# An attention and two-feed-forward kernel on one core: k and q of the first 512 tokens loaded four tokens to a packet, w_out scaled by row, partition maxima turned on DVE

## The chip, the cores and the metric

The kernel runs on 1 core of one Trainium2 chip. The metric is the device time of one execution in microseconds, the median of several runs. TensorE is called PE in the profile (its weight loads PEld), VectorE DVE, ScalarE ACT, GpSimd POOL, SyncE SP.

## What is computed

Four batches of 768 tokens, 8 heads of 64, go through a local attention with 8 memory rows a head, then a gated layer, then a layer with softmax gating and a normalisation. FP32 in and out; the weights come as FP64.

```python
for c in range(nc):                       # chunks of 32 tokens
    k_ctx = k[:, :, c*32-16 : c*32+32+8]  # cut at both ends of the sequence
    k_full = concatenate([mem_k, k_ctx]); v_full = concatenate([mem_v, v_ctx])
    a = softmax(q_c @ k_full.T / 8)
    out[:, :, c*32 : c*32+32] = a @ v_full
x = out as (3072, 512)
y = (sigmoid(x @ w_gate) * (x @ w_val)) @ w_out        # 512 -> 1536 -> 512
h = y @ w_in                                           # 512 -> 1024
solu = h * softmax(h)
out = layernorm(solu) * g_ln @ w2_out                  # 1024 -> 512
```

## The kernel before, in words

The 3072 tokens are 24 tiles of 128 tokens, and 6 blocks of 4 tiles (`j`). There are three stages. In the first, attention makes x of the tiles, and the products with w_gate and w_val run per block over 12 pieces `m` of 128 columns (`up`, line 625: two groups of 12 matmuls with 512 columns, each FP32 product being three with parts `h` and `l`); g = sigmoid times val goes out to DRAM (`gd`). In the second, g comes back and is multiplied with w_out (`down`, line 717). In the third come h (`prod`, line 770, seven products of a two-by-two scheme), the gating and normalisation, and the last product (`out_mm`, line 860).

Attention of a tile `t`: k and q come token by partition (`d_load`, line 472: a descriptor for each token and head, 64 FP32), TensorE turns them four times each with `ident` (`d_turn`, line 456), ACT evicts k into windows of a chunk's 56 tokens plus 8 memory columns (`d_kev`, line 484: three copies) and q (`d_qev`, line 504). POOL copies what neighbours share (`d_halo`) and the memory columns (`d_kmem`). `two_banks` (line 515) makes 32 small matmuls for the scores; DVE takes maximum and difference (`a_max`, lines 530 and 531), ACT the exponential, DVE the sum and its reciprocal (`a_sum`, lines 538 to 540), TensorE turns the result (`d_p`), ACT evicts it (line 547), `two_banks` multiplies with v, DVE divides (`d_norm`, line 593), TensorE turns it (`d_x`), and ACT and DVE split it into `xh` and `xl` (lines 606, 610). v comes as overlapping windows of two tiles (`d_v`, lines 563 to 570), and their tails, the memory rows of v, from a DRAM copy that repeats them eight times (`d_vexp`, `d_vm`, line 582). mem_k is loaded and turned once for each of the four batches (`d_mload`, `d_mem`).

A weight piece is a DMA of 512 KB in 1 KB packets (`w_load`, line 418), an ACT pass for the exponent (`w_exp`, line 214), three DVE operations for the bits (`f32_bits`, lines 219 to 223), an ACT copy for the high part (line 279) and a POOL subtraction for the low one (line 230). w_out also gets a scale: `wo_max` on DVE, `wo_spread` (line 434, an all-reduce over partitions on POOL), `wo_set`. `gm_spread`, `p_spread` and `w2i_spread` are all-reduces too.

The order is not written by hand: `Plan` holds a task for each step with engine, duration, buffers and due times, and lists them all. `SHIFTS` names seeds that move due times at random. Each engine and each DMA queue then runs its list in order.

## Time and profile before

| | us |
|---|---|
| median of 3 runs | 946.63 (945.9 to 946.66) |
| span of the profiled execution, first to last instruction | 944.6 |
| its own time beside the span | not printed; median less span is 2.0 |
| PE busy | 915.7 (97%) |
| DVE busy | 609.3 (65%) |
| ACT busy | 426.6 (45%) |
| POOL busy | 89.2 (9%) |

The profile has the busy time of each engine, the span in slices with the granted clock and the DMA share, the chain of waits that ended last, and groups of instructions by line with what ended the idle time ahead of them. "issue" as releaser means that the profile shows nothing that was waited for. Below, rows of these views are shown word for word.

### The profile page before, as it was taken

Reading aid. Unit: us, or ns where it says so; the run is one execution under the profiler, and the core shown is the slowest. Engines: PE = TensorE matmul, PEld = TensorE weight load, DVE = VectorE, ACT = ScalarE, POOL = GpSimd, SP = SyncE. Lnnn points to the kernel's source line nnn. Section 1 sums busy time; section 2 is a strip of 40 time slices with the busy share of each in tenths; the row PEclk is TensorE's granted clock in tenths of the full one; section 3 lists DMA queues with packets and bytes.
Section 4 is the critical chain, followed back from the end, with each engine's and each line's share of the span. In section 5 each row is a group of like instructions: output and inputs, shape, how many; then the busy total and the mean of one; then the engine's idle time right before and its main releaser. Section 6 shows DMA issues by size and latency. Waiting matters only on the chain.

```text
span 944.6 us, 17813 instructions
## 1 busy us (share of the span) xinstructions
PE 915.7 (97%) x7144; PEld 593.3 (63%) x7144; DVE 609.3 (65%) x1097; ACT 426.6 (45%) x690; POOL 89.2 (9%) x154
## 2 busy tenths in 40 slices
PE   5599999999999999999999999999999999999998
PEld 4487778888888878888787444444444444444443
DVE  3599856656666676677647357783783773777581
ACT  4367632622742462264244245553552633554452
POOL 1143320000100000000006100000000000000000
PEclk9799999999999999999999999999999999999999
DMA  9999997794485557343772532344244144232323
GB/s 175 273 182 219 210 229 243 161 195 152 130 196 172 158 124 199 114 128 122 243 277 85 172 90 78 79 112 101 59 110 101 56 121 94 70 96 45 78 67 101
DMA packets 201746, 132.64 MB, mean 140 GB/s; under 512 B 152768, under 2 KB 167104, under 8 KB 201664
## 3 DMA queue, kind: packets, MB, share of 16 engines
q1 hardware_dynamic: 191424, 105.29, 45.1%
q10 hardware_dynamic: 10240, 26.22, 8.9%
q8 instruction: 56, 0.92, 0.4%
q14 instruction: 26, 0.21, 0.1%
HBM read 86.38 MB, written 33.03 MB: 126 GB/s over the span
## 4 chain that ended last, share of the span: by engine, by line
PE 86%; DVE 5%; DMA 5%; issue 1%; ACT 1%; SPq 1%; POOL 0%; ACTq 0%; DVEq 0%
PE u L625 35%; PE y L717 20%; PE ps L860 13%; PE Q L770 5%; PE tr L456 4%; PE R L770 3%; PE P L770 3%; PE ps L515 3%; DMA r<-in_moe_w_val_dram 2%; DVE w L220 1%; DVE w L223 1%; DVE w L219 1%; DVE pl L401 1%; DMA rk<-in_k_dram 1%; DMA vw<-mv 1%
## 5 line engine op out<-in xcount | busy, mean ns | idle before, releaser
L625 PE MATMUL u<-xh,wa 128*128 128x512 f32 x1152 | 371.1, 396 | 5.1 <-ACT wa L279 1.8
L625 PEld LDWEIGHTS u<-xh,wa 128*128 128x128 f32 x1152 | 216.9, 188 | 53.0 <-ACT sg L631 2.3
L625 PE MATMUL u<-xl,wa 128*128 128x512 f32 x576 | 225.1, 391 | 0.0
L717 PE MATMUL y<-gh,pl 128*128 128x512 f16 x576 | 177.4, 379 | 0.0
L717 PEld LDWEIGHTS <-pl 128*128 128x128 f16 x864 | 84.4, 98 | 102.0 <-issue 0.3
L860 PE MATMUL ps<-wo,nt 128*128 128x512 f16 x576 | 127.6, 379 | 0.8 <-ACT o L867 0.8
L625 PEld LDWEIGHTS u<-xl,wa 128*128 128x128 f32 x576 | 108.7, 189 | 21.4 <-DVE xl L610 0.2
L442 ACT ACTIVATE gh<-gi,gm 128x512 f16<-128x512 f32 x72 | 51.7, 720 | 131.3 <-PE y L717 124.0
L717 PE MATMUL y<-gl,pl 128*128 128x512 f16 x288 | 109.2, 379 | 0.0
L232 DVE SCALAR_TENSOR_TENSOR gl<-gi,gm,gh 128x512 f16<-128x512 f32 x72 | 53.6, 750 | 82.1 <-ACT gh L442 81.9
L860 PEld LDWEIGHTS <-nt 128*128 128x128 f16 x576 | 56.4, 98 | 68.9 <-issue 1.1
L631 ACT ACTIVATE sg<-u 128x512 f32<-128x512 f32 x72 | 42.9, 595 | 123.0 <-PE u L625 108.2
L636 DVE TENSOR_TENSOR g<-sg,u 128x512 f32<-128x512 f32 x72 | 49.3, 685 | 72.9 <-PE u L625 49.4
L770 PEld LDWEIGHTS <-yh 128*128 128x128 f16 x336 | 32.9, 98 | 39.6
L829 POOL TENSOR_TENSOR ls<-ls,mhalf 128x1 f32<-128x1 f32 x24 | 15.4, 645 | 355.4 <-DVE ls L825 355.4
L214 ACT ACTIVATE w<-r 128x512 f32<-128x512 f32 x46 | 30.4, 666 | 36.3 <-DMA r<-in_moe_w_gate_dram 9.5
L770 PE MATMUL Q<-pl,yh 128*128 128x512 f16 x144 | 42.8, 379 | 0.0
L291 DVE TENSOR_REDUCE gm<-g 128x1 f32<-128x512 f32 x60 | 40.9, 681 | 1.7
L219 DVE TENSOR_SCALAR w<-w 128x512 int32<-128x512 int32 x52 | 27.4, 527 | 22.3 <-ACT w L214 22.1
L791 DVE TENSOR_TENSOR pl<-Q,pl 128x512 f32<-128x512 f32 x36 | 24.7, 687 | 23.7 <-PE Q L770 23.6
L230 POOL TENSOR_TENSOR wa<-w,wa 128x512 fp32r<-128x512 f32 x24 | 31.9, 1331 | 76.7 <-ACT wa L279 76.7
L803 ACT ACTIVATE e<-pl,ls,few 128x1024 f32<-128x1024 f32 x24 | 29.7, 1239 | 19.1 <-DVE ls L797 11.8
(122 smaller groups left out, 1112.1 us busy)
## 6 DMA issues: line engine op xcount, KB each, us to landing
gd<-g SPq DMA_DIRECT2D x72, 256.0 KB
gi<-gd SPq DMA_DIRECT2D x72, 256.0 KB
r<-in_moe_w_out_dram ACTq DMA_DIRECT2D x28, 512.0 KB
vw<-in_v_dram SPq DMA_DIRECT2D x64, 98.0 KB
rk<-in_k_dram SPq DMA_DIRECT2D x24, 256.0 KB
...
```

Of the source, the lines that this page charges most:

```text
L219: nc.vector.tensor_single_scalar(out=d, in_=d, scalar=3, op=ALU.logical_shift_left)
L230: nc.gpsimd.tensor_tensor(out=dst, in0=x, in1=hi, op=ALU.subtract)
L232: nc.vector.scalar_tensor_tensor(out=dst, in0=x, scalar=s, in1=hi, op0=ALU.mult, op1=ALU.subtract)
L291: nc.vector.tensor_reduce(out=dst, in_=a, axis=AX.X, op=ALU.max, apply_absolute_value=True)
L442: nc.scalar.activation(out=dst, in_=x, func=AF.Copy, scale=s)
L456: nc.tensor.transpose(pv[:, kk, :], src[:, 2 * kk:2 * kk + 2, :], ident[0:rows, 0:rows])
L625: nc.tensor.matmul(u, lhsT=a, rhs=c[:, kk, w[0]:w[1]], start=(n == 0), stop=(n == 3 * KM - 1))
L631: nc.scalar.activation(out=sg, in_=U.pop((j, m, 0, w)), func=AF.Sigmoid)
L636: nc.vector.tensor_tensor(out=g, in0=U.pop((j, m, "s", w)), in1=U.pop((j, m, 1, w)), op=ALU.mult)
L717: nc.tensor.matmul(y, lhsT=a, rhs=c, start=(f == 0 and n == 0), stop=(f == MF - 1 and n == 2))
L770: nc.tensor.matmul(ps, lhsT=yc[a][:, c, kk, u * 128:(u + 1) * 128], rhs=t[:, hl, kk, :], start=(first and n == 0), stop=(n == 5), skip_gro ...
L860: nc.tensor.matmul(ps, lhsT=nt[:, a, kk, :], rhs=C["wo2"][:, c, kk, :], start=(n == 0), stop=(n == 3 * K2 - 1))
```

## The change

- k and q of tiles 0 to 3 (batch 0, 512 tokens) come in two DMAs each, with four tokens of a head side by side in a partition (1 KB). TensorE turns each head and each of the four tokens with a plain matmul against `ident` (64 columns of weights), not a transpose; the eviction, half on ACT and half on DVE, puts the tokens in order by its read pattern. `kT` windows of these tiles are then full, and `d_halo` has nothing to do for them.
- The first weight pieces stand ahead of v. mem_k of all batches is loaded at once, from ACT's queue, and turned once. The tails of v are made by way of SBUF.
- v gets a 65th column of ones, so the product gives the row sum; `a_sum` is gone, `d_norm` makes the reciprocal.
- w_out's scale is its maximum by row, without the spread; the maxima over all partitions that are left (8) are made by `across` on DVE in 13 small instructions.
- The three DVE steps of a weight piece are tasks of their own; pieces 0 to 19 use four buffers in a place that a later weight takes. `SHIFTS` and due times differ, and `START` sets the first order.

```diff
-    SHIFTS = [(4001, 2), (4002, 0.5), (4006, 0.5), (4010, 2), (4039, 2), (4069, 2), (4114, 1)]
+    SHIFTS = [(2754, 1), (8610, 0.5), (5405, 2), (8526, 0.3), (363, 0.5), (4604, 0.5)]
...
+        for x, n in enumerate(first):
+            T[n]["due"] = x - 100.0
...
-    def wo_spread(f):
-        spread(PF[:, f:f + 1], PF[:, f:f + 1])
-
...
-    def spread(a, dst):
-        nc.gpsimd.partition_all_reduce(dst, a, 128, ReduceOp.max)
+    def across(a):
+
+        nc.vector.tensor_copy(turn[:, 0, 0:1], a)
+        nc.vector.transpose(turn[:, 1], turn[:, 0])
+        nc.vector.tensor_reduce(out=turn[:, 0, 1:2], in_=turn[:, 1], axis=AX.X, op=ALU.max)
+        for x in range(1, 4):
+            nc.vector.tensor_copy(turn[0:1, 0, 1 + x:2 + x], turn[32 * x:32 * x + 1, 0, 1:2])
+        nc.vector.tensor_reduce(out=turn[0:1, 0, 5:6], in_=turn[0:1, 0, 1:5], axis=AX.X, op=ALU.max)
+        for x in range(4):
+            nc.vector.tensor_copy(turn[32 * x:32 * x + 1, 1], turn[0:1, 0, 5:6].to_broadcast([1, 32]))
+        nc.vector.transpose(turn[:, 0], turn[:, 1])
+        nc.vector.tensor_copy(a, turn[:, 0, 0:1])
...
     def d_mload(b):
-        nc.sync.dma_start(out=mm[0:NM], in_=mem_k[b].rearrange("h p d -> p h d"))
+        nc.scalar.dma_start(out=mm[b * NM:(b + 1) * NM], in_=mem_k[b].rearrange("h p d -> p h d"))
...
+    def f_load(nm):
+        R[nm] = xp.tile([128, H, 4, D], F32, tag=dict(rk="xh", rq="xl")[nm], name=nm)
+        src = dict(rk=k, rq=q)[nm][0, :, 0:512, :].rearrange("h (g e) d -> g h (e d)", e=4)
+        for x in range(2):
+            hh = slice(4 * x, 4 * x + 4)
+            nc.sync.dma_start(out=R[nm][:, hh].rearrange("p h e d -> p h (e d)"), in_=src[:, hh])
+
+
+    def f_turn(ps, nm, kk):
+        for e in range(4):
+            for x in range(2):
+                out_ = ps[D * x:D * x + D, e * 128:(e + 1) * 128]
+                nc.tensor.matmul(out_, lhsT=R[nm][:, 2 * kk + x, e, :], rhs=ident, start=True, stop=True)
...
+    def f_kev(t, x):
+        copy = nc.vector.tensor_copy if x else nc.scalar.copy
+        for kk in (2 * x, 2 * x + 1):
+            ps = PS["fk", kk]
+            base = 32 * t - LC // 4
+            for c, n, z in ((0, 1, 10), (1, 3, 14)) if t == 0 else ((0, 3, 14), (3, 1, 12)) if t == 3 else ((0, 4, 14),):
...
+                copy(out_, src)
...
-    def a_sum(t):
-        rs = RS[t] = sm.tile([128, H], F32, tag="rs", name="rs", bufs=4)
-        nc.vector.tensor_reduce(out=rs, in_=SS[t], axis=AX.X, op=ALU.add)
-        nc.vector.tensor_single_scalar(out=rs, in_=rs, scalar=1e-9, op=ALU.add)
-        nc.vector.reciprocal(out=rs, in_=rs)
...
-            w = VW[n] = tp.tile([128, KM, 8, D], F32, tag="vw", name="vw")
+            w = VW[n] = tp.tile([128, KM, 8, D + 1], F32, tag="vw", name="vw")
+            nc.gpsimd.memset(w[..., D:D + 1], 1.0)
...
     def d_norm(t):
...
-        nc.vector.tensor_tensor(out=out_, in0=PS.pop((t, 2)), in1=rs, op=ALU.mult)
+        rs = rs.unsqueeze(3).to_broadcast([128, 2, KM, D])
+        nc.vector.tensor_tensor(out=out_, in0=ps[..., 0:D], in1=rs, op=ALU.mult)
...
+    def gm_top(j):
+        nc.vector.tensor_tensor(out=GM[:, j], in0=GM[:, j], in1=PF, op=ALU.mult)
+        nc.vector.tensor_reduce(out=FH[j], in_=GM[:, j], axis=AX.X, op=ALU.max)
...
+    START = ["vfill", "rk4", "vone"] + [("mload", b) for b in range(B)] + [
+        "rq4", ("dvexp", 0), ("wld", 0), ("wld", 1), ("dv", 0, 0), ("dv", 0, 1), ("dvm", 0), ("rk", 4),
+        ("dv", 1, 0), ("dv", 1, 1), ("dvm", 1), ("wld", 2), "vtwo", ("dvexp", 1)]
```

TensorE's order before, from the start of the program (`rk` and `rq` are k and q by token, `tr` the turned result, `mm` mem_k, `ps` scores or the product with v, `s` the softmax; a count is that of the program, where a plain FP32 matmul stands once):

```order
L456 MATMUL tr<-ident,rk 128x128 x8
L456 MATMUL tr<-ident,mm 128x32 x4
L456 MATMUL tr<-ident,rq 128x128 x8
L515 MATMUL ps<-kT,qT 32x64 x32
L456 MATMUL tr<-ident,rk 128x128 x8
L456 MATMUL tr<-ident,s 128x128 x4
L456 MATMUL tr<-ident,rq 128x128 x4
L515 MATMUL ps<-kT,qT 32x64 x64
L456 MATMUL tr<-ident,rk 128x128 x4
L456 MATMUL tr<-ident,s 128x128 x4
L456 MATMUL tr<-ident,rq 128x128 x4
L515 MATMUL ps<-kT,qT 32x64 x32
```

The same now, twelve rows; eight transposes more and the weight products follow (`fq` is q of the four tiles, in order):

```order
L491 MATMUL tr<-ident,rk 64x128 x32
L491 MATMUL tr<-ident,rq 64x128 x32
L460 MATMUL tr<-ident,mm 128x32 x4
L574 MATMUL ps<-kT,fq 32x64 x96
L460 MATMUL tr<-ident,rk 128x128 x4
L460 MATMUL tr<-ident,s 128x128 x8
L574 MATMUL ps<-kT,fq 32x64 x32
L574 MATMUL ps<-vw,pT 32x65 x32
L460 MATMUL tr<-ident,s 128x128 x4
L574 MATMUL ps<-vw,pT 32x65 x64
L460 MATMUL tr<-ident,s 128x128 x12
L574 MATMUL ps<-vw,pT 32x65 x32
```

The first sixteen transposes of k and q become 64 plain matmuls in one run ahead of everything, and the scores of three tiles follow in one run.

SP's queue before, from the start (`vw` v's windows, `mv` the repeated memory rows of v, `r` a weight piece):

```order
L472 DMA rk<-in_k_dram 128x8x64 x2
L472 DMA rq<-in_q_dram 128x8x64
L460 DMA mm<-in_mem_k_dram 8x8x64
L472 DMA rq<-in_q_dram 128x8x64
L563 DMA vw<-in_v_dram 40x4x64
L570 DMA vw<-in_v_dram 56x7x64 x4
L472 DMA rk<-in_k_dram 128x8x64 x2
L472 DMA rq<-in_q_dram 128x8x64
L577 DMA mv_189<-in_mem_v_dram 512x1x64
L563 DMA vw<-in_v_dram 40x4x64
L570 DMA vw<-in_v_dram 56x7x64 x4
L472 DMA rk<-in_k_dram 128x8x64
```

And now:

```order
L484 DMA rk<-in_k_dram 128x4x256 x2
L484 DMA rq<-in_q_dram 128x4x256 x2
L410 DMA r<-in_moe_w_gate_dram 128x4x256
L410 DMA r<-in_moe_w_val_dram 128x4x256
L617 DMA vw<-in_v_dram 40x4x64
L624 DMA vw<-in_v_dram 56x7x64 x4
L617 DMA vw<-in_v_dram 40x4x64
L624 DMA vw<-in_v_dram 56x7x64 x4
L648 DMA vw<-mv_175 8x4x520 x2
L476 DMA rk<-in_k_dram 128x8x64
L624 DMA vw<-in_v_dram 56x8x64 x8
L648 DMA vw<-mv_175 8x4x520 x2
```

k and q are four issues where they were eight; the first two weight pieces stand ahead of v where they stood behind most of it.

DVE's order now, from its eviction of tiles 1 and 2 on (`wf` a weight piece, `mk` mem_k, `gm` here the maxima of the scores; L527 is the eviction of k, L510 that of q):

```order
L527 COPY kT<-tr 128x4x56 x4
L220 TENSOR_SCALAR wf<-wf 128x512
L223 SCALAR_TENSOR_TENSOR wf<-r,wf 128x512 x2
L510 COPY fq<-tr 128x1024
L470 COPY mk<-tr 128x128
L220 TENSOR_SCALAR wf<-wf 128x512
L223 SCALAR_TENSOR_TENSOR wf<-r,wf 128x512 x2
L586 MEMSET ps 32x2x4x16
L589 TENSOR_REDUCE gm<-ps 128x2x4
L590 TENSOR_TENSOR s<-ps,gm 128x2x4x64
```

Before, DVE began with two memsets, mem_k's copy and the first tile's maximum; two weight pieces and half the evictions now stand ahead of that.

## Rows read from the trace of the kernel before

**Rows 1.** Windows: engines' busy us (instructions), granted clock, DMA share, GB/s, by stage

```profile
0.00:44.40 44.40, 24.61 (x585) 18.50 (x585) 18.54 (x38) 18.32 (x42) 5.24 (x23) 0.88 1.11 222
44.40:130.00 85.60, 82.84 (x875) 67.25 (x876) 74.14 (x114) 54.58 (x101) 33.46 (x40) 0.98 0.95 207
130.00:510.00 380.00, 379.12 (x3705) 309.27 (x3704) 248.15 (x468) 153.12 (x255) 25.19 (x62) 1.00 0.60 171
```

**Rows 2.** Timeline of PE, 4 to 45 us: start, duration, line, count, idle before, releaser

```profile
4.20 2.23 PE L456 MATMUL tr<-ident,rk 128*128 128x128 f32 x8 [4.20 <-DMA rk<-in_k_dram]
...
14.71 1.06 PE L456 MATMUL tr<-ident,s 128*128 128x128 f32 x4
...
18.99 0.32 PE L515 MATMUL ps<-kT,qT 64*32 64x64 f32 x8 [0.77 <-issue]
...
20.37 0.60 PE L456 MATMUL tr<-ident,s 128*128 128x128 f32 x4
...
22.87 0.85 PE L515 MATMUL ps<-kT,qT 64*32 64x64 f32 x64 [0.82 <-ACT qT L504]
...
25.93 0.64 PE L515 MATMUL ps<-vw,pT 64*32 64x64 f32 x39 [0.23 <-DMA vw<-mv]
29.13 0.65 PE L515 MATMUL ps<-vw,pT 64*32 64x64 f32 x23 [2.56 <-issue]
...
36.83 0.48 PE L515 MATMUL ps<-vw,pT 64*32 64x64 f32 x33 [3.03 <-issue]
...
39.40 1.11 PE L456 MATMUL tr<-ident,s 128*128 128x128 f32 x4
...
44.39 0.77 PE L625 MATMUL u<-xh,wa 128*128 128x512 f32 x1 [1.82 <-ACT wa L279]
```

**Rows 3.** Waits of PE, whole run: total us, times, longest

```profile
PE ps L515 <- issue: 6.4, 3, 3.0
```

**Rows 4.** Page, parts 1 and 3: TensorE's instructions, and the queue of instruction packets

```profile
PE 915.7 (97%) x7144; PEld 593.3 (63%) x7144; DVE 609.3 (65%) x1097; ACT 426.6 (45%) x690; POOL 89.2 (9%) x154
...
q8 instruction: 56, 0.92, 0.4%
```

**Rows 5.** DMA queues in one-us stretches from 15.5, 25.5, 33.5, 40.5 us: packets, MB, share

```profile
q8 instruction: 1, 0.02, 9.3%
q8 instruction: 1, 0.02, 8.0%
q8 instruction: 1, 0.02, 7.2%
q8 instruction: 1, 0.02, 7.1%
```

**Rows 6.** Windows of 2 us, columns as in rows 1

```profile
16.00:18.00 2.00, 2.00 (x122) 1.59 (x122) 0.47 (x1) 1.12 (x3) 0.00 (x1) 1.00 1.33 167
38.00:40.00 2.00, 2.00 (x69) 1.55 (x68) 0.60 (x2) 0.58 (x1) 0.00 (x0) 0.50 1.09 348
```

**Rows 7.** Timeline of SP's queue and ACT, 20 to 28 us

```profile
20.12 0.71 SPq L582 DMA_DIRECT2D vw<-mv  x2
20.88 0.39 SPq L418 DMA_DIRECT2D r<-in_moe_w_gate_dram  x1
...
27.44 0.66 ACT L214 ACTIVATE w<-r 128x512 f32<-128x512 f32 x1 [4.19 <-DMA r<-in_moe_w_gate_dram]
```

**Rows 8.** Groups of DVE by form: busy us, mean ns of one, idle before

```profile
L220 DVE SCALAR_TENSOR_TENSOR w<-r,w 128x512 int32<-128x512 int32 x46 | 33.7, 733 | 1.6
...
L531 DVE TENSOR_TENSOR s<-ps,smx 128x512 f32<-128x512 f32 x24 | 16.6, 692 | 0.8
...
L538 DVE TENSOR_REDUCE rs<-s 128x8 f32<-128x512 f32 x24 | 16.1, 671 | 3.2 <-ACT s L534 3.2
...
L438 DVE TENSOR_SCALAR pf<-pf 128x1 f32<-128x1 f32 x12 | 1.8, 151 | 3.8 <-POOL pf L434 3.8
```

**Rows 9.** Timeline of PE at the second batch's mem_k

```profile
77.03 0.43 PE L456 MATMUL tr<-ident,mm 32*128 32x32 f32 x4
```

More of the change, by code (lines that the diff above doesn't have):

```diff
@@ L7 @@
 from concourse._compat import with_exitstack
-from concourse.bass_isa import ReduceOp
 from concourse.masks import make_identity
@@ L44, in add, with order @@
         )
-    def order(self):
+    def order(self, first):
         T = self.tasks
@@ L170, in encoder_kernel, with column @@
     const = ctx.enter_context(tc.tile_pool(name="const", bufs=1))
+    turn = const.tile([128, 2, 32], F32, name="turn")
+    tiny = const.tile([128, 2 * MF + 4 * K2 + 18], F32, name="tiny")
+    ends = [0]
+    def column(n):
+        ends.append(ends[-1] + n)
+        return tiny[:, ends[-2]:ends[-1]]
+    gcol, PM, PW, GS = (column(K2) for x in range(4))
+    PF, SF = column(MF), column(MF)
+    fo, mhalf, few = column(1), column(1), column(16)
     wpool = ctx.enter_context(tc.tile_pool(name="wpool", bufs=1))
@@ L179, in encoder_kernel @@
     dr = ctx.enter_context(tc.tile_pool(name="dr", bufs=1, space=DRAM))
-    gcol = const.tile([128, K2], F32, name="gcol")
-    fo = const.tile([128, 1], F32, name="fo")
-    mk = [const.tile([128, KM, NM], F32, name=f"mk{b}") for b in range(B)]
     FIRST_IN = {6: ("w", 0), 8: ("w", 1), 10: ("w", 2)}
@@ L189, in encoder_kernel @@
     FIRST_TAGS = {f"wa{m}" for m in FIRST_IN}
-    wa = [None if m in FIRST_IN else wpool.tile([128, 2, 2, 512], F32R, name=f"wa{m}") for m in range(MF)]
+    WF = 20
+    FIRST_TAGS |= {f"wa{MF - 1}", f"wa{MF - 3}"}
+    wa = [None if f"wa{m}" in FIRST_TAGS else wpool.tile([128, 2, 2, 512], F32R, name=f"wa{m}") for m in range(MF)]
     def slot(x, shape, dt=F32):
@@ L888, in one @@
             prev=(nm, t - 1), **kw)
-    add("zero", POOL, 0.5, d_zero)
     add("ident", POOL, 0.7, d_ident)
     for b in range(B):
-        one("mload", b, SP, 0.1, d_mload, [("dmem", b - 1) if b else "zero"], dma=[0.09])
-        one("dmem", b, PE, 0.3, d_mem, ["ident", "mload"], acq=[("u0", ("dm", b))])
-        one("dmev", b, DVE, 0.3, d_mev, ["dmem"], rel=[("u0", ("dm", b))])
+        one("mload", b, ACT, 0.1, d_mload, dma=[0.09], acq=[] if b else [("g", "mm")])
+    add("dmem", PE, 0.3, d_mem, deps=["ident"] + [("mload", b) for b in range(B)], acq=[("a", "dm")], rel=[("g", "mm")])
+    add("dmev", DVE, 0.2, d_mev, deps=["dmem"], rel=[("a", "dm")])
     for n in range(NTILE // 2):
@@ new lines, in encoder_kernel @@
+        one("dhalo", t, POOL, 0.6, d_halo, after + ([("dhalo", t - 1)] if i else []) + ([("dkev2", 3)] if t == 4 else []))
+        one("dkmem", t, POOL, 0.45, d_kmem, after + ["dmev"])
+        one("sw", t, PE, 0.85 if early else 0.75, d_scores,
+            (["fqev0", "fqev1", "dkev", "dkev2"] if early else ["dqev"]) + ["dkmem", ("dhalo", t if i == TB - 1 or t < 3 else t + 1)],
+            acq=[("a", t), ("s", t)], rel=[("kT", t)] + ([("qT", t)] if t > 3 else [(f"wa{MF - 3}", "early")] if t == 3 else []), slack=0 if t < 6 else SLACK)
@@ L963, in encoder_kernel @@
             continue
-        one("wexp", n, ACT, 0.68, w_exp, ["wld"], acq=[("w", n)])
-        one("wbits", n, DVE, 2.2, w_bits, ["wexp"], rel=rel)
-        one("whi", n, ACT, 0.62, w_hi, ["wbits"], acq=[(f"wa{m}", m)] if m in FIRST_IN and n % 2 == 0 else [])
-        one("wlo", n, POOL, 1.4, w_lo, ["whi"], rel=[("w", n)])
+        buf = [("wf" if n < WF else "w", n)]
+        one("wexp", n, ACT, 0.68, w_exp, ["wld"], acq=buf + ([(f"wa{MF - 1}", "wf")] if n == 0 else []))
+        for x, y in enumerate(("wsh", "wlow", "wbits")):
+            one(y, n, DVE, (0.46, 0.74, 0.74)[x], lambda n, x=x: w_bits(n, x), [("wexp", "wsh", "wlow")[x]], rel=rel if x == 2 else [])
+        one("whi", n, ACT, 0.62, w_hi, ["wbits"], acq=[(f"wa{m}", m)] if f"wa{m}" in FIRST_TAGS and n % 2 == 0 else [])
+        one("wlo", n, POOL, 1.4, w_lo, ["whi"], rel=buf + ([(f"wa{MF - 1}", "wf")] if n == WF - 1 else []))
     for f in range(MF):
@@ L1033, in encoder_kernel @@
     add("gcol", SP, 0.1, lambda: nc.sync.dma_start(out=gcol, in_=g_ln.rearrange("(k p) -> p k", p=128)), dma=[0.1])
-    add("mhalf", DVE, 0.07, lambda: nc.vector.memset(mhalf, -0.5))
+    add("turn", DVE, 0.07, lambda: nc.vector.memset(turn, 0.0), due=0.1)
+    add("mhalf", DVE, 0.07, lambda: nc.vector.memset(mhalf, -0.5), due=0.1)
+    add("warm", ACT, 0.2, warm, deps=["mhalf"], table="exp", due=1.0)
     add("w2done", "mark", 0, lambda: None, deps=[("tlo", c) for c in range(7)])
@@ L1127, in encoder_kernel @@
         plan.tasks[n]["due"] = clock
+    line = [n for n in START if plan.tasks[n]["eng"] == SP]
+    for a, b in zip(line, line[1:]):
+        plan.tasks[b]["prev"] = a
+    plan.tasks["rq4"]["prev"] = ("mload", B - 1)
     ctx.enter_context(tc.manual_schedule())
-    for part in plan.order():
+    for part in plan.order(START):
         part["fn"]()
```

207 lines of the change are left out of this document (125 added, 82 removed).

## The prediction

> **What bounds the kernel now.** I read the stages first, then TensorE's own order, then what ended its idle time. By stages [rows 1], TensorE is busy 82.8 of the 85.6 us from 44.4 to 130 and 379.1 of the 380 up to 510; the weight products fill it from 44.4 us on. In the first 44.4 us it works 24.6, though the DMA engines are full (a share of 1.11). So the place where the change can pay is the road to the first weight product, which starts at 44.39 [rows 2]. I call that moment T0. What shortens it comes off the end one for one, since after it nothing but TensorE's own work sets the end; what the change saves on DVE, ACT or POOL later is cover.
>
> What holds T0? Three lines of TensorE end idle time put down to "issue", in which nothing the profile follows is waited for: 0.77 us before 18.99, 2.56 before 29.13, 3.03 before 36.83 [rows 2]. They cut a run of equal matmuls in the middle, and TensorE's list of waits has no others of the kind in the whole run [rows 3]. Counted over all lines of that stretch, 220 pairs of weight load and matmul stand before the first stop, 125 more before the second, 126 more before the third. The page gives 7144 pairs and, on the queue named "instruction", 56 packets of 0.92 MB, 16.4 KB each [rows 4]: 7144 / 56 = 127.6 pairs to a packet. So TensorE's program comes in pieces of some 126 pairs, and these are the stops where the next piece was not there. Such packets are seen in the one-us stretches that begin at 15.5, 25.5, 33.5 and 40.5 [rows 5]: each of the first three ends some 2.5 to 3 us before the matmul that waited. From the start of one piece to the start of the next, a piece took 18.99 to 29.13 = 10.1 us and 29.13 to 36.83 = 7.7; the one before took 4.3 (its predecessor began, by the count, near the line at 14.71). I call this a refill.
>
> The rest of the time before T0 is data. Packets of 256 B, of which k, q and v come (64 FP32 of a head and token), move 167 GB/s, the 1 KB packets of the weights 348 [rows 6]. The small tail of v issued at 20.12 lets the first product with v begin at 25.93, and the first weight piece, issued at 20.88, is used at 27.44 [rows 2, 7].
>
> **The change, part by part.** Load: k and q of tiles 0 to 3 are 2.1 MB; at 167 GB/s that is 12.6 us of the engines, at 348 6.0, so 6.6 us less in front of v and the weights. Laid end to end in SP's new order, with 2 us to the first bytes: k and q 6.0, weights 0 and 1 3.0, the small loads 1, v of the first pair with its tail 1.0 MB 6.0, a k tile 1.6, v of the second pair 1.0 MB 6.2; v of tiles 2 and 3 is in near 26. I allow 1 us to land: 27. It serves the third product, the old counterpart of which went on at 36.83.
>
> Turning: 32 transposes of 128 columns go, 64 plain matmuls with 64 columns of weights come. Plain FP32 matmuls stand twice in the trace (64 pairs of them for a tile, 32 in the program), so 128 pairs replace 32. No row shows one. A transpose takes 0.60 / 4 = 0.15 us at full clock, 1.11 / 4 = 0.28 at 39.40, where the granted clock is 0.50, the 1.2 GHz of the two levels [rows 2, 6]. Below, they cost what the 32 did, 4.8 us; above, each pair costs a whole transpose, 19.2. I take half of the latter, 9.6, because each fills half the columns: from 4.2 (where the first turn starts now [rows 2]) to about 14. The evictions of k and q, now ACT's, become halves on ACT and DVE; six halves at 0.69 [rows 8], 4 us, come to DVE before T0, where it is busy 18.5 of 44.4 [rows 1].
>
> Scores, maximum and exponential of four tiles: DVE needs two operations of 0.69 a tile plus two weight pieces of three operations near 0.73 [rows 8], which the new order puts ahead of the first maximum. Laid in a row, scores of tile 1 run near 16.5 and those of tile 3 near 22.5, the last product with v near 28, and then its division (0.69 and two small ones), a transpose of 0.6 and the copy that feeds the weight product, with DVE's other work between: T0 near 33 by the engines alone; by the data, 27 and the 7.56 from 36.83 to 44.39, it is 34 to 35. I take 34 for both.
>
> The refills come in again there. By the count, 584 pairs lie before T0 now and 680 then (96 more). The pieces' ends at 220, 345, 471 and 596 pairs fall in tile 1's scores (16.5), early in tile 3's scores, at the start of the second product with v, and right behind the third. **Three refills thus stand between 16.5 and the last stretch, where now two do.** What one takes in the new traffic isn't shown; its ends are 4.3 and 10.1. I take 6.0: nearer the low end, since from 26 us on only 1 KB packets are queued, and under those the packet at 40.5 to 41.5 [rows 5] starts at most 4.7 us after 36.83. Three give 16.5 + 18.0 = 34.5; the last stretch (two transposes, a product of 0.85 or more [rows 2], a division, a transpose, a copy) 5.0: **T0 = 39.5**, 4.9 us earlier.
>
> The rule that speaks here is in the Trainium skill, DMA: Bandwidth & Descriptors, section Queues, rings and completion order: each DMA engine takes the queues that have work in turn, packet by packet. By that a refill would wait for a packet or so and never for the backlog, and T0 would be 34; the rows with 7 us between 18.99 and the packet's stretch from 25.5 do not look like it. This is the first rival.
>
> After T0: three turns of mem_k go (once for all batches), 0.43 each, a little of it under what follows: 1.1 off [rows 9]. The ones column makes 65 columns of 64 in the products of 20 later tiles; between nothing and 1/64 of 0.85 each, I take 20 x 0.013 = 0.3 on. The row sums leave DVE, 24 x 0.67 = 16 us; 20 all-reduces leave POOL, and 8 turns come to DVE, 13 small instructions each. At 0.15, a small one of the present [rows 8], that is 16 us; its ends are nothing and, at 0.69, 72. All under TensorE: from 130 to 510 us DVE is idle 132 of 380 [rows 1], so the upper end is covered too unless it sits in one place. Six DMAs go to ACT's queue ahead of its first copy; that copy can't come before the first turns end, past 5 us, so nothing. SP's tail of v now waits for mem_v to go to SBUF and out to DRAM, and a k tile and the second v stand behind it; some 8 us for two trips against a turn at 12 or later: nothing.
>
> Sum on the profiled execution: 944.6 - 4.9 - 1.1 + 0.3 = 938.9. Its span is 944.6, the median of the runs 946.63, so 2.0 lie around it: **940.9**. What a measurement of this kernel can tell from no change is 0.2%, 1.9 us.
>
> **The rivals.** *Refills never late.* They wait for a packet, not a queue; then T0 = 34 and 944.6 - 10.4 - 0.8 + 2.0 = 935.4. For: behind 36.83 no stop follows [rows 3], though TensorE goes on through its pieces. Against: three in the first 37 us. If the 2.8 us that TensorE idles from 44.4 to 130 shrink too, 932.6; this is the low end, with 1.6 for a quicker turning. 0.25.
>
> *Weights late.* T0 moves, but from 44.4 to 130 DVE works 74.1 of 85.6 [rows 1] at weight pieces and four tiles, so the block ends no sooner than DVE lets it: four row sums, 2.7, and the 0.8: 943.1. Against: TensorE is the fuller of the two. 0.07.
>
> *Refills as now.* The mean of the three is 7.4; four of them from the turning's first piece end (9.8) and the last stretch give 9.8 + 29.6 + 5.0 = 44.4: T0 stays, and 945.8. 0.18.
>
> *Slower: refills as the longest.* The 96 added pairs put one more refill in the road. At 10.1 each, T0 = 9.8 + 40.4 + 5.0 = 55.2, and 956.6. It decides from 8.2 us a refill on, where T0 is 47.6 and the time 949. For it: the longest is the one in a queue of v's 256 B packets, and v is what is queued when the third is due. Against: two of three were shorter, and weights fill the queue by then. 0.14, most of it just past the point.
>
> **How the numbers follow.** The forecast case has 0.36, and with it the others give faster 0.36 + 0.25 + 0.07 = 0.68, same 0.18, slower 0.14. The range takes in the first rival with its low end and reaches up to the point where the last begins to decide, 931 to 949; about 0.15 is outside. The faster cases alone span 931 to 944.
>
> **What would show it.** Right: T0 at 38 to 41; SP's k and q by 9 us at some 340 GB/s; stops put down to "issue" 125 pairs apart, four of them, before T0; refill packets that precede them by 3 us; TensorE full from T0 on with its busy time within 1 us of now after it. Wrong: no such stops before T0 (first rival), T0 at 44 or later with stops of 4 us and more (the last two), or idle TensorE between T0 and T0 + 70 put down to ACT or POOL at the weights (the second). A turning of over 15 us would break the step on its price, TensorE waiting for v near 30 us that on the load. A stop in the later blocks at the small DVE turns would break the cover.

## The result, and the profile after

The changed kernel takes **960.33 us** (median of 4 runs, 956.95 to 965.35); the kernel before, beside it on the same chip, 946.64 (945.90 to 947.54). The ratio is 1.0143, interval 1.011 to 1.0176: 1.4% slower, where 940.9 was forecast. The profiled execution took 956.95 with a span of 954.7, so 2.3 us lie around it; it is the fastest of the four. Two executions below, one of the changed kernel in another order (1060.41 us) and one of the kernel before (1055.23), ran at a granted clock of 0.84 and are left out of the ratios.

The stages, with the columns of [rows 1]:

```profile
0.00:44.40 44.40, 25.24 (x679) 22.30 (x680) 21.66 (x51) 16.97 (x38) 6.25 (x19) 0.80 1.07 228
44.40:130.00 85.60, 80.15 (x844) 64.16 (x843) 69.94 (x104) 51.70 (x90) 32.92 (x37) 0.95 0.86 193
130.00:510.00 380.00, 372.57 (x3679) 305.93 (x3678) 239.16 (x500) 144.57 (x255) 12.31 (x55) 1.00 0.62 174
```

TensorE's first number in the second and third line is what to read: 80.15 of 85.6 where it was 82.84, and 372.57 of 380 where it was 379.12 [rows 1]. Most of the loss against the kernel before lies where the prediction had said that nothing could be lost. The road to the first weight product, TensorE's timeline from 4 to 46 us as in [rows 2]:

```profile
4.98 5.86 PE L491 MATMUL tr<-ident,rk 128*64 128x128 f32 x64 [4.98 <-DMA rk<-in_k_dram]
10.65 3.67 PE L491 MATMUL tr<-ident,rq 128*64 128x128 f32 x64
...
16.86 1.60 PE L574 MATMUL ps<-kT,fq 64*32 64x64 f32 x128 [2.17 <-POOL kT L555]
19.96 1.17 PE L574 MATMUL ps<-kT,fq 64*32 64x64 f32 x64 [1.51 <-DVE s L590]
24.03 1.08 PE L460 MATMUL tr<-ident,rk 128*128 128x128 f32 x4 [2.89 <-DMA rk<-in_k_dram]
...
26.82 1.11 PE L460 MATMUL tr<-ident,s 128*128 128x128 f32 x4 [0.85 <-ACT s L593]
...
32.33 1.57 PE L574 MATMUL ps<-vw,pT 64*32 64x65 f32 x123 [1.38 <-issue]
33.84 0.66 PE L460 MATMUL tr<-ident,s 128*128 128x128 f32 x4
39.02 1.87 PE L460 MATMUL tr<-ident,s 128*128 128x128 f32 x8 [4.52 <-issue]
...
45.68 0.79 PE L694 MATMUL u<-xh,wa 128*128 128x512 f32 x1 [0.68 <-ACT xh L675]
```

T0 is 45.68, not earlier than before (44.39) though k and q are turned by 14.3. Behind it, TensorE's list of waits over the whole run:

```profile
PE tr L460 <- issue: 5.2, 2, 4.5
...
PE ps L574 <- issue: 4.3, 2, 2.9
PE u L694 <- ACT sg L700: 4.1, 1, 4.1
```

Three of these are behind T0: 4.10 us at 74.62 (for ACT's sigmoid), and 0.66 before 269.20 and 2.93 before 276.91, both put down to "issue". From T0 to the last product with w_gate and w_val (it ends at 530 us, in the kernel before at 523) TensorE idles 12.3 us in the changed kernel and 4.5 in the kernel before.

### The profile page after: what moved, and what is told of

The parts are those of the page before. It is cut to its first block, busy times and chain, and to the rows that moved or that the text cites. A ratio compares the mean times of both kernels' runs of the same rounds, so it can differ in the third digit from the quotient of the medians.

```text
span 954.7 us, 18077 instructions
## 1 busy us (share of the span) xinstructions
PE 918.0 (96%) x7228; PEld 598.2 (63%) x7228; DVE 617.2 (65%) x1188; ACT 416.7 (44%) x678; POOL 85.5 (9%) x140
## 3 DMA queue, kind: packets, MB, share of 16 engines
q1 hardware_dynamic: 184000, 105.02, 44.4%
## 4 chain that ended last, share of the span: by engine, by line
PE 85%; DMA 5%; DVE 5%; SPq 2%; issue 1%; ACT 1%; DVEq 0%; ACTq 0%
PE u L694 35%; PE y L788 20%; PE ps L931 13%; PE Q L841 5%; PE tr L460 3%; PE R L841 3%; PE P L841 3%; PE ps L574 3%; DMA vw<-in_v_dram 2%; DVE wf L223 2%; DMA r<-in_moe_w_val_dram 1%; DMA mv<-mv 1%; SPq L624 1%; DMA tiny<-in_moe_g_ln_dram 1%; DVE pl L393 1%
## 5 line engine op out<-in xcount | busy, mean ns | idle before, releaser
L900 POOL TENSOR_TENSOR ls<-ls,tiny 128x1 f32<-128x1 f32 x24 | 18.1, 758 | 385.0 <-DVE ls L896 351.2
L223 DVE SCALAR_TENSOR_TENSOR w<-r,w 128x512 int32<-128x512 int32 x64 | 47.1, 736 | 2.2
L862 DVE TENSOR_TENSOR pl<-Q,pl 128x512 f32<-128x512 f32 x36 | 24.7, 687 | 27.0 <-PE Q L841 26.9
L460 PE MATMUL tr<-ident,s 128*128 128x128 f32 x192 | 31.7, 298 | 9.2 <-issue 5.2
L938 ACT ACTIVATE o<-ps,tiny 128x512 f32<-128x512 f32 x24 | 16.5, 686 | 44.1 <-PE ps L931 44.1
L874 ACT ACTIVATE e<-pl,ls,tiny 128x1024 f32<-128x1024 f32 x24 | 29.6, 1235 | 10.7 <-DVE ls L883 7.3
```

The lines of the kernel that those rows point to most:

```text
L223: nc.vector.scalar_tensor_tensor(out=d, in0=a, scalar=n, in1=d, op0=op, op1=ALU.bitwise_or)
L460: nc.tensor.transpose(pv[:, kk, :], src[:, 2 * kk:2 * kk + 2, :], ident[0:rows, 0:rows])
L874: nc.scalar.activation(out=e, in_=h, func=AF.Exp, bias=s[:, 0:1], scale=FH[j], accum_out=s[:, 1:2])
```

## The experiments

"Stops" below are idle times of TensorE in its timeline. T0 is the start of the first weight product. Each median stands beside runs of the kernel before on the same chip, and the ratio is to those.

**1. The load and turn undone; v's rows wider; two other draws of the order.** The planner adds random shifts to its due times, from a list of seeds (SHIFTS), before it draws the order; the change replaced that list and a slack. First kernel, cut to its core:

```diff
-    START = ["vfill", "rk4", "vone"] + ...
+    START = ["vfill", ("rk", 0), ("rk", 1), "vone"] + ...
-        if t < 4:
+        if t < 0:
```

> The changed kernel with k and q of the first four tiles loaded and turned as in the kernel before (256 B packets, 32 transposes), all else as changed. Road theory (the loss sits in front of the first weight product, because 96 more pairs cost a refill): the time comes back to 947 to 951 us, first weight product near 42 to 44. Column theory (v's packets into rows of 65 columns are slower, and v holds the road): the load still pays its part, the first weight product comes later than 45.7, time 958 or more. Order theory (the drawn order of the stages after the first weight product decides): the stalls at 70 and 270 us move, by chance, 945 to 965.

Measured: 947.45 us, ratio 0.9991 (0.9977 to 1.0005). T0 is 47.42, *later* than in the changed kernel, and no stop longer than 0.9 us stands behind it. Its windows:

```profile
44.40:130.00 85.60, 82.20 (x854) 65.84 (x854) 67.43 (x107) 51.87 (x92) 33.16 (x37) 0.94 0.98 220
130.00:530.00 400.00, 398.59 (x3796) 323.93 (x3795) 258.42 (x515) 156.00 (x270) 28.80 (x60) 1.00 0.61 173
```

In this order the whole slowdown goes with the load and turn, as the road theory's time wanted, but not by the road: that theory wanted T0 at 42 to 44. The rest of the change (ones column, row scales, turns on DVE, mem_k once) adds nothing that can be measured in this order. Undoing a part also draws another order, though, and section 5 shows what that alone is worth.

```diff
-            w = VW[n] = tp.tile([128, KM, 8, D + 1], F32, tag="vw", name="vw")
+            w = VW[n] = tp.tile([128, KM, 8, 72], F32, tag="vw", name="vw")
...
```

> The changed kernel, v's windows in SBUF with rows of 72 columns (288 B apart) in place of 65 (260 B); the products still read 65. Column theory: v's 256 B packets go from about 35 to 49 ns each between 14 and 26 us back to some 30, the data of tile 4 lands near 22 in place of 24, first weight product 1 to 3 us earlier, time 954 to 958. Road by refills and order theory: within 2 us of the changed kernel, 957 to 962, packets as slow as before.

Measured: 959.06 us, ratio 1.0116 (1.0086 to 1.0145), T0 45.13. DMA queues from 20 to 26 us, packets, MB and share of 16 engines, in the changed kernel and then in this one:

```profile
q1 hardware_dynamic: 3078, 0.82, 125.5%
```

```profile
q1 hardware_dynamic: 3369, 0.85, 93.6%
```

A packet took 1.255 x 16 x 6000 ns / 3078 = 39 ns of an engine, and takes 27 here. The packets behaved as the column theory said, yet hardly more bytes moved, k of tile 4 was still waited for until 24.09, and the time stayed within the band of the other theories. The width of v's rows is not the cause.

```diff
-    SHIFTS = [(2754, 1), (8610, 0.5), (5405, 2), (8526, 0.3), (363, 0.5), (4604, 0.5)]
+    SHIFTS = []
```

> The changed kernel with no random shifts of the due times (the list SHIFTS empty): same work, another order. Order theory: the 4.1 us stop at 70 us and the two stops of 4.3 us in all near 270 go or move, time anywhere from 943 to 970, and not within 3 us of 960. Road theory: the road up to 45 us is set by a fixed list, so first weight product at 45 to 47, and the time within 4 us of 960.

Measured: 959.9 us, ratio 1.0124 (1.0084 to 1.0163): within the band of the road theory, and within the 3 us of 960 that the order theory had ruled out. But the stops moved, as the order theory said: 2.69 at 73.09, 0.96 at 179, 1.57 at 274, 2.08 at 353, 1.39 at 440.

```diff
+    SHIFTS = [(4001, 2), (4002, 0.5), (4006, 0.5), (4010, 2), (4039, 2), (4069, 2), (4114, 1)]
-    FIRST, RATE, LEAD, SLACK, EARLY, LATER = 30.0, 1.12, 30.0, 1.0, 140.0, 235.0
+    FIRST, RATE, LEAD, SLACK, EARLY, LATER = 30.0, 1.12, 30.0, 3.0, 140.0, 235.0
```

> The changed kernel with the random shifts and the slack of the kernel before. Order theory: another draw, anywhere from 943 to 970, with other stops after 60 us. Road theory: first weight product at 45 to 47, time within 4 us of 960.

Measured: 952.99 us, ratio 1.0042 (1.0021 to 1.0062). T0 is 47.10; there is a stop of 3.13 at 77.98 and none put down to "issue" behind T0. The same work in another order is 7 us faster with a *later* T0, below the band of the road theory.

**2. The stop at 74 us: order or load?** ACT's timeline in the changed kernel, start, duration and what ended the wait:

```profile
67.18 0.62 ACT L280 CAST wa<-wf 128x512 fp32r<-128x512 f32 x1 [1.52 <-DVE wf L223]
70.58 0.62 ACT L280 CAST wa<-wf 128x512 fp32r<-128x512 f32 x1 [2.78 <-DVE wf L223]
73.45 0.62 ACT L280 CAST wa<-wf 128x512 fp32r<-128x512 f32 x1 [2.25 <-DVE wf L223]
73.97 0.59 ACT L700 ACTIVATE sg<-u 128x512 f32<-128x512 f32 x1
```

The sigmoid that TensorE waits for could have run near 67; it stands behind casts that wait for DVE. DVE's groups from 44 to 76 us (busy, mean ns) show why these come late:

```profile
L223 DVE SCALAR_TENSOR_TENSOR wf<-slot,wf 128x512 int32<-128x512 int32 x12 | 11.2, 948 | 0.1
L220 DVE TENSOR_SCALAR wf<-wf 128x512 int32<-128x512 int32 x10 | 8.6, 858 | 0.3 <-ACT wf L214 0.3
```

The same operations take 0.68 and 0.41 when POOL rests. DVE's timeline has both prices of L220, and POOL's has the subtraction (L228) that ran beside the second:

```profile
62.90 0.41 DVE L220 TENSOR_SCALAR wf<-wf 128x512 int32<-128x512 int32 x1
68.43 1.52 DVE L220 TENSOR_SCALAR wf<-wf 128x512 int32<-128x512 int32 x1
```

```profile
67.88 1.79 POOL L228 TENSOR_TENSOR wa<-wf,wa 128x512 fp32r<-128x512 f32 x1 [1.19 <-ACT wa L280]
```

L220 at 68.43 ended at 69.95, the subtraction at 69.67. The Trainium skill (SBUF — State Buffer, Terms) states that DVE and GpSimd arbitrate for a port pair that is locked for a whole instruction while the loser blocks; the rows agree, with 1.52 - 0.41 = 1.1 us for this collision.

In the list that the planner returns, one part is put ahead of another before the instructions are written:

```diff
...
+        (("sig", 0, 3, (0, 512)), ("whi", 10)),
...
```

> The changed kernel with one instruction moved: on ACT the sigmoid of the fourth weight product of the first block stands ahead of the two casts of weights (pieces 10 and 11) behind which it stood. ACT-order theory (the stop of 4.1 us at 74.6 is the sigmoid queued behind casts that wait for DVE, while the weights of the next product were ready at 69.7): the stop shrinks below 1 us, TensorE goes on near 70.5 at full clock, and the end comes 4 to 5.5 us earlier, 955 to 956. Weights theory (the pieces are late, whatever the order): a stop of 2 us or more stays or comes back one product later, and the time stays within 2 us of 960.

Measured: 959.72 us, ratio 1.012 (1.0088 to 1.0151). The stop did not go; it became 2.68 at 74.77, for ACT's next instruction, the copy of tile 5's k:

```profile
74.77 0.66 PE L460 MATMUL tr<-ident,rk 128*128 128x128 f32 x4 [2.68 <-ACT kT L540]
```

That copy was moved too:

```diff
...
+        (("sig", 0, 3, (0, 512)), ("whi", 10)),
+        (("up", 0, 3, 1, (0, 512)), ("whi", 10)),
+        (("dk", 5), ("whi", 10)),
+        (("dkev", 5), ("whi", 10)),
...
```

> The changed kernel with, on ACT, the sigmoid of the fourth weight product and the copies of tile 5's k out of PSUM ahead of the two casts of weight pieces 10 and 11 (and on TensorE's side nothing reordered). With the sigmoid alone moved, the stop became one of 2.7 us for that copy. ACT-order theory: both stops go, none over 1 us between 50 and 130 us, and at 130 us the weight products stand 5 us further than in the changed kernel. The end comes 5 us earlier, 954 to 956, if TensorE's work sets it from there; if it is given back at the stops for TensorE's program near 270 and 350, as with the sigmoid alone, those grow by 3 us or more and the time stays at 957 to 960.

Measured: 958.74 us, ratio 1.0118 (1.0068 to 1.0168). Again the next one in ACT's line:

```profile
80.81 0.86 PE L574 MATMUL ps<-kT,qT 64*32 64x64 f32 x64 [3.25 <-ACT qT L562]
```

So the order on ACT is not it. Then one of DVE's three operations on a weight piece was left out, with the order kept; the kernel then leaves out the low bits of the weights:

```diff
-        f32_bits(w, raw_, (x,))
+        f32_bits(w, raw_, (x,) if x != 1 else ())
```

> The changed kernel without the middle one of the three DVE operations on each of the 24 weight pieces of the gate and value products (the low bits of the unpacking are left out); the order of all others is the same. Weights theory (DVE is the bound from the first weight product to 75 us, 9.8 of 10 us busy): the stop at 74 us goes, DVE is under 9 of 10 us there, and the time falls by 4 to 6 us, to 954 to 956. Theory of the later refills (the loss is the 4.3 us near 270 and what the runs scatter by): the time falls by less than 2 us.

Measured: 952.21 us, ratio 1.0059 (1.0037 to 1.0082): 8 us off by the medians, 4.5 by the spans of the profiled executions (950.2 for 954.7), and no stop over 0.3 us from T0 to 129. Windows 44.4 to 70 and 70 to 80 us of the changed kernel, and then of this one (columns as in rows 1):

```profile
44.40:70.00 25.60, 24.93 (x100) 19.81 (x99) 24.79 (x33) 12.08 (x19) 12.27 (x10) 0.88 0.81 165
70.00:80.00 10.00, 5.90 (x26) 4.72 (x25) 8.31 (x11) 5.54 (x14) 5.73 (x9) 0.83 1.05 242
```

```profile
44.40:70.00 25.60, 24.69 (x103) 20.01 (x103) 17.79 (x28) 14.45 (x25) 14.07 (x12) 0.93 0.99 220
70.00:80.00 10.00, 10.00 (x111) 8.13 (x111) 5.41 (x10) 7.47 (x17) 4.56 (x8) 1.00 1.19 232
```

DVE falls from 24.79 of 25.6 to 17.79, and TensorE rises from 5.90 of 10 to 10.00. Between T0 and 75 us DVE is the bound of the changed kernel, and its work on the weights the load that makes it so. That explains this stop and not the whole loss: from 130 to 530 us TensorE idles 9.3 us here, and 7.5 in the changed kernel. What the same cut is worth in the kernel before was not tried. After the 4.1 us of idling TensorE also restarts slowly: the mean granted clock from 74 to 76 us is 0.57, near the lower of its two levels (0.50).

**3. The road itself.**

```diff
-        ("wld", 0), ("wld", 1), ("dv", 0, 0), ("dv", 0, 1), ("dvm", 0), ("rk", 4),
+        ("rk", 4), ("wld", 0), ("wld", 1), ("dv", 0, 0), ("dv", 0, 1), ("dvm", 0),
```

> The changed kernel with the load of k of tile 4 issued ahead of the first weights and the first v, in place of behind them. It tests the step of the prediction that what shortens the road to the first weight product comes off the end one for one. Data: the wait of 2.9 us for k of tile 4 at 24.0 goes, and the first weight product comes 1 to 3 us earlier, unless a refill or v takes the place (then within 1 us of 45.7). One for one: the end moves by what the first weight product moves, 957 to 959 us. Weights theory: the end stays at 959 to 962 whatever the first product does, and the stop near 70 to 74 grows by as much.

Measured: 957.59 us, ratio 1.0122 (1.0086 to 1.0157), T0 43.60, 2.1 us earlier. The stop at 71 is 2.92 us, others went to 95 (2.84) and 260 to 271. The median is inside the one-for-one band, but the profiled span is 955.2 against 954.7 and the intervals overlap: this run by itself decides nothing. In the two profiled executions nothing came off the end: the last product with w_gate and w_val starts at 529.96 here and at 529.77 in the changed kernel.

```diff
-        KT[t] = ktp.tile([128, KM, 4, 64], F32, tag="kT", name="kT")
+        KT[t] = ktp.tile([128, KM, 4, 64], mybir.dt.bfloat16, tag="kT", name="kT")
...
```

> The changed kernel with k and q rounded to bf16 on the way out of PSUM, so that a score product is one pair of weight load and matmul in place of two: 64 pairs fewer a tile, 1536 of 7228 in all, 256 of the 680 before the first weight product. It leaves precision out. A score pair takes 13 ns at full clock, so TensorE itself saves up to 64 x 24 x 0.013 = 20 us if a bf16 pair costs the same. Refill theory (126 pairs to a packet of TensorE's program, stops where it is late): about 45 instruction packets in place of 57, one stop before the first weight product in place of two, that product 3 to 6 us earlier, no stop near 270. If the stops are something else (v late, a semaphore not shown), they stay at 1 to 5 us at the same products with v. The time falls by TensorE's own saving and the stops, to 935 to 950.

Measured: 946.29 us, ratio 0.999 (0.9972 to 1.0009). From the page, TensorE's instructions and the packets of its program, in the changed kernel and then here:

```profile
PE 918.0 (96%) x7228; PEld 598.2 (63%) x7228; DVE 617.2 (65%) x1188; ACT 416.7 (44%) x678; POOL 85.5 (9%) x140
...
q8 instruction: 57, 0.93, 0.4%
```

```profile
PE 907.2 (96%) x6460; PEld 587.7 (62%) x6460; DVE 614.6 (65%) x1188; ACT 415.2 (44%) x678; POOL 86.0 (9%) x140
...
q8 instruction: 51, 0.84, 0.4%
```

768 pairs went, not the 1536 of the expectation (a score product stood as two pairs and now stands as one: 32 fewer a tile), and 6 packets: 128 pairs to a packet. One stop before T0 in place of two, T0 at 43.08. So much is as the refill theory said. The stops near 270 stayed, though (0.59 and 2.64). The span fell by 11.1 us: T0 came 2.6 earlier, TensorE works 10.0 less behind it (0.8 more of its saving lies before T0 and is part of the 2.6), and it idles 1.5 more there. So of the 2.6 us on the road 1.1 came off the end.

**4. The stop near 270 us.** In the changed kernel, TensorE's timeline there:

```profile
269.20 1.20 PE L460 MATMUL tr<-ident,s 128*128 128x128 f32 x9 [0.66 <-issue]
270.24 0.60 PE L460 MATMUL tr<-ident,rk 128*128 128x128 f32 x4
270.70 0.66 PE L460 MATMUL tr<-ident,rq 128*128 128x128 f32 x4
272.10 0.66 PE L460 MATMUL tr<-ident,s 128*128 128x128 f32 x4 [0.75 <-ACT kT L540]
272.69 1.29 PE L574 MATMUL ps<-vw,pT 64*32 64x65 f32 x105
276.91 0.43 PE L574 MATMUL ps<-vw,pT 64*32 64x65 f32 x23 [2.93 <-issue]
```

9 + 4 + 4 + 4 + 105 = 126 pairs between two stops, done in 4.8 us, and the next piece of the program begins 7.7 us after the last.

```diff
...
+        (("up", 2, 7, 0, (0, 512)), ("pv", 14)),
...
```

> The changed kernel with one piece of TensorE's order moved: the first half of the eighth weight product of the third block (12 pairs, 2.7 us) stands ahead of the products with v of tiles 14 and 15 instead of behind them. Between 269.20 and 273.98 us 126 pairs of tile work run in 4.8 us, and the next run of pairs begins 7.7 us after the last one began. Refill theory: the stop of 2.9 us at 276.91 shrinks below 0.8, TensorE works where it waited, and the end comes 2 to 3 us earlier, 957 to 958. Rival (v of tiles 14 and 15 or a buffer is what is late, the view only does not show it): the same stop stands behind the weight product or goes with the wait for v; if it stays, 960; a stop that stays at the same place within the product with v, 126 pairs after the last, at 2 us or more refutes the sum of the refill.

Measured: 961.74 us, ratio 1.0152 (1.0112 to 1.0192). The stop went entirely. The two products with v now run through:

```profile
275.73 1.49 PE L574 MATMUL ps<-vw,pT 64*32 64x65 f32 x128
277.91 0.63 PE L460 MATMUL tr<-ident,s 128*128 128x128 f32 x4 [0.69 <-DVE s L662]
...
283.31 0.50 PE L694 MATMUL u<-xh,wa 128*128 128x512 f32 x1 [1.59 <-DVE xl L679]
```

This alone does not refute the rival, since 2.7 us of work put ahead would also have covered a v that is late. The kernel with bf16 scores speaks against it: there, too, 7 + 4 + 4 + 4 + 107 = 126 pairs stand between the two stops, and the second falls after 107 of the 128 pairs with v, where it fell after 105. The stop goes with the count of pairs and not with a piece of v:

```profile
264.60 1.31 PE L574 MATMUL ps<-vw,pT 64*32 64x65 f32 x107
268.55 0.42 PE L574 MATMUL ps<-vw,pT 64*32 64x65 f32 x21 [2.64 <-issue]
```

What was saved did not come off the end. 0.69 and 1.59 us went to waits for DVE just behind, and stops put down to "issue" of 2.2 us in all stand from 345 to 358, which the changed kernel's profile does not have. These last can't be put down to the move: the profiles with ACT's sigmoid moved and with v's rows wider, where nothing near 270 was touched, have 2.0 and 1.8 us of them at 345 to 354.

Then this move, those of ACT's order and a third:

```diff
...
+        (("up", 3, 6, 0, (0, 512)), ("pv", 18)),
...
```

> Both moves together, and a third like the first: half of the seventh weight product of the fourth block ahead of the product with v of tile 18, where 2 us of stops stood near 350 in some runs. If the three places make up what the changed kernel loses against the kernel before, the time is 947 to 951. If the loss is somewhere else, or moves on, 954 or more.

Measured: 960.6 us, ratio 1.0124 (1.0092 to 1.0157), T0 48.00. A miss: the three places, mended by hand, do not make up the loss. It moves on.

**5. Is it the draw?** With the load and turn undone everything came back; but that also drew another order. So the program without them, and the kernel before, were drawn again. Only the lines on SHIFTS (and the slack that goes with them) differ, as in the two diffs of that kind above; the last of the four is

```diff
-    SHIFTS = [(4001, 2), (4002, 0.5), (4006, 0.5), (4010, 2), (4039, 2), (4069, 2), (4114, 1)]
+    SHIFTS = [(2754, 1), (8610, 0.5), (5405, 2), (8526, 0.3), (363, 0.5), (4604, 0.5)]
-    FIRST, RATE, LEAD, SLACK, EARLY, LATER = 30.0, 1.12, 30.0, 3.0, 140.0, 235.0
+    FIRST, RATE, LEAD, SLACK, EARLY, LATER = 30.0, 1.12, 30.0, 1.0, 140.0, 235.0
```

> The changed kernel with k and q of the first tiles loaded and turned as before, and with no random shifts. Structure theory (the load and turn cost time in any order): 945 to 950, as the same program under the changed kernel's shifts (947.4). Draw theory (an order costs or saves up to 10 us by chance): anywhere from 945 to 962, and 952 or more in at least one of this and the next.

> The changed kernel with k and q of the first tiles loaded and turned as before, and with the shifts and the slack of the kernel before. Structure theory: 945 to 950. Draw theory: anywhere from 945 to 962.

> The kernel before with no random shifts, its work the same. Structure theory: 945 to 950, the shifts are worth 3 us at most. Draw theory: 950 to 960, with stops at 70 to 130 us or put down to issue after 130 us.

> The kernel before with the shifts and the slack of the changed kernel. Structure theory: 945 to 950. Draw theory: 950 to 960.

Measured medians: 948.84, 954.72, 955.65 and **967.64** us; ratios 1.0007 (0.9996 to 1.0019), 1.0066 (1.0046 to 1.0087), 1.0085 (1.0069 to 1.01) and 1.021 (1.0194 to 1.0225). Windows of the kernel before with the changed kernel's shifts (TensorE's busy us and instructions, granted clock, DMA share, GB/s):

```profile
44.40:130.00 85.60, 74.38 (x817) 0.90 0.98 210
130.00:530.00 400.00, 396.00 (x3783) 1.00 0.59 169
```

The kernel before, not a line of its work changed, is 2.1%, some 20 us, slower in another order. All nine, by program and draw (profiled run: T0; TensorE's busy time from 44.4 to 130 and idle time from 130 to 530, all in us):

| program | shifts | median | ratio | T0 | busy to 130 | idle to 530 |
|---|---|---|---|---|---|---|
| before | its own | 946.64 | 1 | 44.39 | 82.84 | 1.7 |
| before | none | 955.65 | 1.0085 | 44.93 | 78.94 | 3.1 |
| before | of the change | 967.64 | 1.021 | 45.22 | 74.38 | 4.0 |
| change without load and turn | of the change | 947.45 | 0.9991 | 47.42 | 82.20 | 1.4 |
| same | none | 948.84 | 1.0007 | 45.60 | 81.91 | 3.2 |
| same | of before | 954.72 | 1.0066 | 45.24 | 75.98 | 2.1 |
| change | its own | 960.33 | 1.0143 | 45.68 | 80.15 | 7.5 |
| change | none | 959.9 | 1.0124 | 45.18 | 79.99 | 9.2 |
| change | of before | 952.99 | 1.0042 | 47.10 | 78.41 | 2.4 |

Structure theory falls: the draws of one program lie 0.75% to 2.1% apart, 7 to 20 us. At equal shifts the ratios with and without the load and turn differ by 0.0152, 0.0117 and -0.0024: 14, 11 and -2 us, and in the last pair the intervals overlap. T0 tells nothing of the order of the medians.

A full DVE behind T0 does not tell slow from fast either. Windows 44.4 to 70 us (columns as in rows 1) of the kernel before, and of the change without load and turn and without shifts:

```profile
44.40:70.00 25.60, 25.37 (x172) 20.64 (x173) 24.67 (x33) 15.03 (x30) 12.04 (x13) 0.94 0.94 191
```

```profile
44.40:70.00 25.60, 24.59 (x100) 19.50 (x99) 25.05 (x32) 11.82 (x19) 11.70 (x10) 0.89 1.05 219
```

Both are among the fast ones with DVE at 24.67 and 25.05 us of 25.6, and in the second TensorE also waits 2.13 us at 72.63 for ACT's sigmoid.

**6. A planner that knows.** Two corrections: measured costs of DVE's operations, and 126 pairs to take 7.5 us at least.

```diff
-        one(y, n, DVE, (0.46, 0.74, 0.74)[x], ...
+        one(y, n, DVE, (0.66, 0.95, 0.95)[x], ...
...
+                    if used + p > bound:
+                        u = max(u, begun + 7.5 - t["dur"] * (bound - used) / p)
...
```

> The changed kernel, its planner booking the measured 0.66, 0.95 and 0.95 us for the three DVE operations on a weight piece, and letting no run of TensorE pass the end of 126 pairs sooner than 7.5 us after it began. If the stops come from an order planned on wrong costs: no stop over 1 us put down to issue after 130 us, none over 2 us at 70 to 80, 946 to 953. If DVE, ACT and POOL simply have no more to give between 45 and 130 us, or the draw is chance: 953 to 965.

> The same planner for the changed kernel with k and q of the first tiles loaded and turned as before. If the planner's costs matter: 943 to 947, under the kernel before. If chance: 946 to 956.

> The kernel of the last line without the rule on pieces, the measured DVE costs alone: tells which of the two corrections does it. If costs: 943 to 948; if chance: 946 to 956.

Measured: 957.38 us (ratio 1.0091, 1.0067 to 1.0115), 981.52 (1.0349, 1.0324 to 1.0374) and 958.89 (1.0117, 1.0087 to 1.0147). In the first no stop is put down to "issue" behind T0, as the rule on pieces meant; but the order that it drew brought k of the next tile late:

```profile
52.04 1.12 PE L471 MATMUL tr<-ident,rk 128*128 128x128 f32 x4 [8.85 <-DMA rk<-in_k_dram]
```

That wait stands ahead of T0, which is 57.57 here, 11.9 us later than in the changed kernel, and yet the span is only 1.1 longer (955.8). From T0 to the end this order takes 898.2 us, where the changed kernel takes 909.0 and the kernel before 900.2 (11 pairs more stand ahead of T0 here than in the changed kernel): behind T0 the loss is gone, and the road has taken its place.

The other two, 981.52 and 958.89 against 947.45, are worse than the same program under the old costs, and both lie above the bands of both theories: for this program better costs in the planner did not give better orders. That an order's cost is chance is not shown by this; why 981.52 is so slow was not followed up (behind T0, TensorE's longest waits there are for DVE, up to 4.7 us). With the rule on pieces neither program has a stop put down to "issue" behind T0; without it there is one of 1.82 us at 350. No version was found that is faster than the kernel before.

## Why the prediction was wrong

*The road to T0: right in kind, 6.2 us too early.* Loading came as put: 330 GB/s from 4 to 10 us. The turning took 5.86 + 3.67 = 9.5 us against 9.6, in part by luck: k's half cost 92 ns a pair and q's 57, both at a granted clock of 1.00, and the 75 of the forecast is their mean and neither of them. Of the four pieces of the program that end before T0, only the last two end in a stop (1.38 and 4.52 us), at 473 and 600 pairs, by the count over the timeline, against 471 and 596; the one that can be timed lasts 39.02 - 32.33 = 6.7 us against 6.0. (In the kernel before, the instruction packets end 2.3 to 2.6 us ahead of the matmul that waited, not 2.5 to 3.) The first rival, with no refill late and T0 at 34, does not describe these rows. The miss is made of three terms. The piece that begins at 32.33 was put at 16.5 + 12.0 = 28.5: 3.8 us, because between 14.7 and 27 us TensorE waited 2.17 + 1.51 + 2.89 + 0.85 us for POOL's mem_k columns, DVE, k of tile 4 and ACT, and v moved 136 GB/s from 20 to 26 where 167 was taken. The refill was 0.7 longer. The last stretch took 6.7 for 5.0, at a granted clock of 0.50, the lower level.

*The step that failed: "What shortens it comes off the end one for one, since after it nothing but TensorE's own work sets the end; what the change saves on DVE, ACT or POOL later is cover."* The runs refute the first half: in the table above T0 goes from 44.4 to 47.4 and the medians from 947 to 968, unrelated, and behind T0 TensorE waits 12.3 us up to 530, where the forecast left it the 4.5 of the kernel before; with bf16 scores 1.1 of 2.6 us came off the end, and under the corrected planner a T0 11.9 us later put the end off by 1.1. The second half was read from 82.84 of 85.6 us [rows 1], an average over a stage: from T0 to 70 us DVE works 24.67 of 25.6 in the kernel before too. There it is no cover but level with TensorE, and its operations were priced at 0.73 us [rows 8], the mean of the run, where they take 0.86 to 0.97 in the stretch in which POOL works on the weights beside them. The experiment that took one of them away removed the stop and 4.5 us of the profiled execution (8 of the median); reordering did not. The rival "weights late" named the place, with the wrong sign and 0.07.

*The step that was not there: the redraw.* SHIFTS and the slack stand in the diff, and the sum gave them no term. The runs price it: by the ratios up to 20 us for the kernel before, 7 for the change without load and turn and 10 for the change. The kernel before sits at the best of its three draws. In hindsight, a term of "0 to 20 us, upwards" would have moved the forecast from faster to slower; that it points upwards could be known only by drawing the kernel before again.

*The slower rival* wanted refills of 10.1 us before T0. The one that can be timed took 6.7. The rival named the wrong place: late pieces stop TensorE behind T0 as well, where tile work is drawn close together, which "no others of the kind in the whole run" [rows 3] had made me rule out. That held for one order, not for the program.

*In sum*, on the profiled execution: 956.95 - 940.9 = 16.0 us, of which 6.2 T0, 12.3 - 4.5 = 7.8 more idle time between T0 and the last product with w_gate and w_val, and 2.0 left. Behind T0 TensorE is busy 1.0 us longer than in the kernel before, where 0.8 less was forecast; it restarts at a granted clock of 0.50 at 46 to 50 us (0.81 in the kernel before) and 0.57 at 74 to 78 (1.00). The median lies 3.4 above that execution; why the runs of the changed kernel scatter by 8 us, and those of the kernel before beside them by 1.6, was not settled. The stops at 345 to 358 us, which stand in some profiles and not in others, are one sign of it.

*Open:* whether the load and turn cost time by themselves. Two draws of three say 11 and 14 us, one says -2; three draws are few, and what makes one order slower than another was not traced to one cause. That DVE's extra halves of the evictions before T0 are what puts it behind was not tried.
